# Second S buffer, spaced conversion steps and another conversion order in the first tile of an attention and feed-forward kernel

## The chip, the cores and the metric

The kernel runs on one core of one Trainium2 chip. The metric is device time in microseconds (us) of one execution; lower is better. An engine's instructions run in the order of its own queue, and an instruction waits at the head of that queue for what it needs, so that all behind it waits too. The engines are named as in the profile: PE (matmul), PEld (its weight loads), DVE (vector), ACT (scalar), POOL, and SP, which issues the DMAs.

## The reference, cut to what matters

```python
def _attn_ref(q, k, v, tau):                      # q, k, v: (4, 6080, 256)
    qn = q / (np.linalg.norm(q, axis=1, keepdims=True) + 1e-06)
    kn = k / (np.linalg.norm(k, axis=1, keepdims=True) + 1e-06)
    s = kn.transpose(0, 2, 1) @ qn / tau          # (4, 256, 256)
    a = softmax(s)                                # over the last axis
    return v @ a

def _moe_ref(x, w_in, w_out):                     # x: (24320, 256), d_ff 2048
    h = x @ w_in
    g = np.maximum(0.01 * h, h)
    return g @ w_out
```

`w_in` and `w_out` arrive as 64-bit floats; everything else is 32-bit.

## The kernel before, in words

For each of the 4 batches the kernel forms the 256x256 attention matrix, multiplies it into `w_in` (one 256x2048 weight per batch), and then runs `v` through this weight, the leaky step and `w_out`. Every operand of a matmul is split into a high and a low part, and a product is made of three passes (high-high, low-high, high-low), each a matmul of 128x128 by 128x512.

**Tiles and blocks.** The rows of a batch are cut into tiles of 1024. A tile passes through 8 blocks (the loop over `p`, 0 to 7). From tile 1 on a block is computed with seven weight combinations (A11, A12, A22 and the sums S1 to S4: a Strassen form, lines 978 to 1010). Tile 0, the first tile of the first batch, is computed directly (lines 963 to 975): a block has four products, C11 in bank x, C22 in bank y, C21 in bank z and C12 in bank x again. Each product has six matmuls (line 606). ACT then applies the leaky step out of the bank (`leaky`, line 617) and casts the high part (line 618), and DVE takes the low part (line 620). The products with `w_out` of a block (24 matmuls, line 653) are issued between the products of the next block in pieces of 5, 5, 8 and 6. Bank x is therefore wanted by C11 of the next block only 6 matmuls after C12 has filled it.

**Weights of the first batch.** The attention matrix times `w_in` is made in four pieces j = 0 to 3 of 512 columns, each of two halves h (`w_product`, line 421, six matmuls a half; here "W product"). Blocks 2j and 2j+1 of tile 0 use piece j: `direct_high` (ACT, line 433) and `direct_low` (DVE, line 437) copy it out of its bank into a buffer of the tag `w_split`. Pieces 2 and 3 also go to DRAM for later tiles, as all pieces do: `direct_store` stores the A parts, and `direct_sum` and `w_parts` (lines 443, 477) form S1 to S4 out of them, split them (ACT line 489, DVE line 490) into a tile `w_rest` with one buffer, and store that (line 502) once for each of the two blocks k = 0, 1 of the piece.

**Conversions.** The 64-bit weights are converted on the chip in pieces of 128x512 by seven steps (`f64_steps`): exponent (DVE, line 328), scaled (ACT, 333), tailed (ACT, 336), signed (DVE, 339 and 342), joined (DVE, 345 and 346), high part (ACT, 352) and low part (DVE, 355). A raw piece lies in one of four buffers (`raw`), which its low part frees. Four pieces of `w_in` are converted before tile 0; eight pieces `("wo", i)` of `w_out` and four `("win", j, h)` follow within it. Blocks 2j and 2j+1 need wo 2j+1, then wo 2j.

**The order.** Inside tile 0 the extra work stands in queues `todo` for "act", "dve", "pe" and "pe_late", as entries of a length, a function and a rank. `put` inserts by rank. After each product, `slot(queue, room)` issues entries from the front of a queue while the first one fits into the room. `steps_work` puts one step of a conversion and, once that is issued, the next one. `convert` and `direct_work` start conversions and S sums at given blocks. The recorded order is what each engine runs.

Of the kernel before, what the change touches and what calls it, by code (L numbers as in the profile page):

```python
# [10 lines left out]
F32R = mybir.dt.float32r  # L11
# [6 lines left out]
P = 128  # L18
# [13 lines left out]
def channel_attention_ffn(  # L32
# [36 lines left out]
    work = ctx.enter_context(tc.tile_pool(name="work", bufs=2))  # L69
# [4 lines left out]
    def bank(tag, bufs=1):  # L74
        return psum.tile([P, TW], F32, name="ps_" + tag, tag=tag, bufs=bufs)
# [15 lines left out]
    wo = [wo_hl[:, x:x + NF * C].rearrange("p (f d) -> p f d", d=C) for x in (0, NF * C + P)]  # L91
# [273 lines left out]
    win = {}  # L365
# [69 lines left out]
    def direct_low(j, h):  # L435
        hi, lo = w_direct[j, h]
        return nc.vector.tensor_tensor(out=lo, in0=a_sb[0, j, h], in1=f32(hi), op=ALU.subtract)
# [18 lines left out]
    def w_tmp(name):  # L456
        return work.tile([P, TW], F32, name=name, tag="w_tmp", bufs=4)
# [9 lines left out]
    def w_parts(b, j):  # L467

        HT = TW // 2
        a = [a_sb[b, j, h] for h in range(CH)]  # L470
        a21, a11, a22, a12 = a[0][:, 0:HT], a[0][:, HT:TW], a[1][:, 0:HT], a[1][:, HT:TW]
        s12, s34 = w_tmp("w_s"), w_tmp("w_s")
        s1, s2, s3, s4 = s12[:, 0:HT], s12[:, HT:TW], s34[:, 0:HT], s34[:, HT:TW]

        def sums(*of):
            for out, x, y, op in of:
                last = nc.vector.tensor_tensor(out=out, in0=x, in1=y, op=op)
            return last

        yield 0.8, lambda: sums((s1, a21, a22, ALU.add), (s3, a11, a21, ALU.subtract))  # L480
        yield 0.8, lambda: sums((s2, s1, a11, ALU.subtract), (s4, a12, s2, ALU.subtract))
        two = "p (s f) -> p s f"

        def split(k, to, at, *blocks):
            ks = slice(k * P, (k + 1) * P)
            for src, x0, n in blocks:
                src = src[:, ks] if n == 1 else src.rearrange(two, s=2)[:, :, ks]
                hi, lo = (x[:, x0 - at, :] if n == 1 else x[:, x0 - at:x0 - at + n, :] for x in to)
                (nc.vector.tensor_copy if b else nc.scalar.copy)(out=hi, in_=src)
                last = nc.vector.tensor_tensor(out=lo, in0=src, in1=f32(hi), op=ALU.subtract)  # L490
            return last

        for k in range(2):
            p, w = 2 * j + k, []

            def blocks(x0, n, name, w=w):

                w.append(work.tile([P, 2, n, P], F32R, name=name, bufs=1))
                return [w[-1][:, x] for x in range(2)]

            def store(x0, n, w=w, p=p):
                nc.sync.dma_start(
                    out=w_dram[b, p][:, :, x0 * P:(x0 + n) * P], in_=f32(w[-1].rearrange("p x s f -> p x (s f)"))
                )

            def begin(k=k, blocks=blocks, store=store):
                x0 = min(A11, A22)
                last = split(k, blocks(x0, 3, "w_first"), x0, (a11, A11, 1), (a[1], A22, 2))
                store(x0, 3)
                return last  # L510
# [160 lines left out]
    todo = {"act": deque(), "dve": deque(), "pe": deque(), "pe_late": deque(), "pe_next": deque()}  # L671
    steps = {}

    def at(w, fn, *args):
        steps.setdefault(w, []).append((fn, args))

    def slot(queue, room):
        engine = queue.split("_")[0]
        while todo[queue] and todo[queue][0][0] <= room:
            length, fn, _ = todo[queue].popleft()  # L680
            room -= length
            with in_order(engine):
                ins = fn()
            issued[engine] = ins

    def put(queue, length, fn, then=(), first=False):


        def run():
            ins = fn()  # L690
            for entry in then:
                if entry[0] == "call":
                    entry[1](*entry[2:])
                else:
                    put(*entry)
            return ins

        rank = 0 if first is True else first or 99
        at = 0 if first is True else sum(x[2] <= rank for x in todo[queue])
        todo[queue].insert(at, (length, run, rank))  # L700

    scores = [Scores(b, [G] * (NCHUNK // G)) for b in range(B)]

# [34 lines left out]
    def w_work(b, j, h=0):  # L738


        def taken():
            ins = w_taken(b, j, h)
            if h == 0:
                w_work(b, j, 1)
            else:
                for length, fn in w_parts(b, j):
                    put("dve", length, fn)
                if j + 1 < NWC:
                    length, fn, _ = todo["dve"].pop()
# [28 lines left out]
        put("dve", 0.7, lambda: direct_sum(j, 0), (), rank)  # L778
        put("dve", 0.7, lambda: direct_sum(j, 1), [("call", parts)], rank)

    def steps_work(rank, steps, then=()):
        (engine, length, fn), *rest = steps
        put(engine, length, fn, [("call", steps_work, rank, rest, then)] if rest else then, rank)

    def v_work(i, n0, n1, first=False):
        entries = v_entries[i][n0:n1]
        for length, fn in reversed(entries) if first else entries:
            put("dve", length, fn, (), first)

    v_entries, late = {}, {}  # L790

    def v_begin(i):
        v_entries[i] = list(v_parts(i))
# [2 lines left out]
    for i in range(NTILES):  # L796
        w = i * NPAIR
# [9 lines left out]
    conversions = deque([("wo", 1), ("wo", 0), ("win", 2, 0), ("win", 2, 1), ("wo", 2), ("wo", 3), ("win", 3, 0),  # L807
                         ("win", 3, 1), ("wo", 4), ("wo", 5), ("wo", 6), ("wo", 7)])
    loaded = deque()

    def convert_load(n=1):
# [5 lines left out]
    def convert(n):  # L817

        late["wanted"] = late.get("wanted", 0) + n
        while late["wanted"] and loaded:  # L820
            late["wanted"] -= 1
            of, steps = loaded.popleft()
            then = [("call", convert_load)]
            if len(of) == 2 and of[1] == CH - 1:
                then.append(("call", w_early, of[0], 0))
            late["rank"] = late.get("rank", 0) + 1
            steps_work(late["rank"], steps, then)

    for w, *calls in (
        (0, (convert, len(conversions) - 1), (direct_work, 0, 3, 3), (w_early, 1, 0)),  # L830
        (2, (direct_work, 1, 5, 9)),
        (6, (direct_work, 2, 50, 50)),
        (7, (direct_work, 3, 50, 50)),
    ):
        for fn, *args in calls:
            at(w, fn, *args)
# [83 lines left out]
    parts = [fn for _, fn in v_parts(0)]  # L920
    wo_first = [fn for engine, _, fn in loaded.popleft()[1]]
# [12 lines left out]
    ordered("dve", wo_first[0], parts[2], sc.turned_low)  # L934
    wo_first[1]()
    wo_first[2]()
    for h in range(CH):
        ordered("pe", lambda: w_product(0, 0, h, "yz"[h]))
        direct_high(0, h)
        ordered("dve", (parts[3], wo_first[4])[h], lambda: direct_low(0, h))  # L940
        if h == 0:
            ordered("dve", wo_first[3])
    fill(FILL * G)
    wo_first[5]()
    ordered("dve", wo_first[6])

    outs = []
# [9 lines left out]
    for i in range(NTILES):  # L957
        for p in range(NPAIR):
# [3 lines left out]
                fn(*args)  # L962
            if i == 0:
                for tag, (name, x, y), n in zip("xyzx", BLOCKS, (5, 5, 8, 24)):
                    ps = bank(tag)
                    direct_product(p, ps, x, y)
                    slot("act", 1.4)
                    out(n)
                    late["bank"] = "z" if tag == "x" else "y"
                    slot("pe_late", 0 if n == 5 else 1)  # L970
                    leaky(i, p, name, ps, temp(name="h"))
                    slot("act", 0.7)
                    slot("dve", 2.6)
# [68 lines left out]
```

## Time and profile before

| | |
|---|---|
| median of 3 runs | 2229.51 us (2229.44 to 2230.23) |
| the profiled execution, its own time | 2228.81 us |
| its span, first to last instruction | 2227.0 us |
| busy: PE, DVE, ACT | 98%, 66%, 66% |
| mean granted TensorE clock | 0.991 |
| tile 0 on PE, first product of block 0 to first product of tile 1 | 66.68 to 196.26 us |

The span is 1.81 us shorter than the execution's own time. Rows of the timeline give the start, the length, the engine, the line, the operation, what it writes and reads, the number of merged instructions, and in square brackets how long the engine had been idle and what released it. A row of the windows gives for a stretch its length and each engine's busy time (with the number of instructions), then the granted clock of PE, the DMA share and GB/s.

### The profile page before, as it was taken

The numbers are of one execution on the slowest core, as the hardware profiler recorded it, in microseconds if no ns is written. First come the engines' busy times: TensorE is split into PE (matmuls) and PEld (weight loads), VectorE is DVE, ScalarE is ACT, GpSimd is POOL, SyncE is SP. The second block draws the span as 40 slices with busy tenths as digits, with TensorE's granted clock in tenths as the row PEclk, the third lists the DMA queues.
The fourth block names the chain that finished last, engine by engine and source line by source line (L and its number), as shares of the span: only waits on it lengthen the run. The fifth ranks groups of instructions, "written<-read, shape, count | busy, mean of one in ns | idle before, by whom it ended". The sixth has DMA issues, their size and how long they took to land.

```text
span 2227.0 us, 27287 instructions
## 1 busy us (share of the span) xinstructions
PE 2177.6 (98%) x9960; PEld 1819.0 (82%) x9960; DVE 1464.8 (66%) x2572; ACT 1479.1 (66%) x2564; POOL 3.3 (0%) x11
## 2 busy tenths in 40 slices
PE   9787999999999999999999999999999999999999
PEld 7566888888888888888888888888888788888888
DVE  7666776766676766666767667667577555556554
ACT  6455777766667777776656777777666666666665
POOL 0000000000000000000000000000000000000000
PEclk9899999999999999999999999999999999999999
DMA  9535443442753434433465344343354432332331
GB/s 346 181 127 194 145 165 129 142 151 89 233 203 121 152 119 144 157 119 139 146 225 172 111 154 159 121 157 131 111 193 155 146 137 83 137 121 94 125 114 39
DMA packets 108533, 327.75 MB, mean 147 GB/s; under 512 B 10992, under 2 KB 29296, under 8 KB 108400
## 3 DMA queue, kind: packets, MB, share of 16 engines
q1 hardware_dynamic: 108400, 326.02, 42.7%
q8 instruction: 78, 1.28, 0.2%
q14 instruction: 55, 0.45, 0.1%
HBM read 267.52 MB, written 58.46 MB: 146 GB/s over the span
## 4 chain that ended last, share of the span: by engine, by line
PE 90%; DVE 4%; DMA 2%; ACT 2%; issue 1%; SPq 0%; ACTq 0%; DVEq 0%
PE ps_o L653 44%; PE ps_x L593 22%; PE ps_z L593 11%; PE ps_y L593 5%; PE ps_s L180 4%; PE ps_s L421 1%; DMA w_dram<-w_rest 1%; ACT h L617 1%; DVE g_split L620 1%; ACT g_split L618 1%; PE ps_x L606 1%; DVE h L627 1%; DMA qk_raw<-in_k_dram 1%; DVE sq_acc L140 0%; DVE w_rest L490 0%
## 5 line engine op out<-in xcount | busy, mean ns | idle before, releaser
L653 PE MATMUL ps_o<-g_split,w_out_split 128*128 128x512 f32 (+1 forms) x4608 | 1167.0, 389 | 0.7 <-DVE w_out_split L355 0.7
L653 PEld LDWEIGHTS ps_o<-g_split,w_out_split 128*128 128x128 f32 x4608 | 868.1, 188 | 177.0 <-DVE w_out_split L355 1.1
L620 DVE TENSOR_TENSOR g_split<-h,g_split 128x512 fp32r<-128x512 f32 (+1 forms) x768 | 525.2, 684 | 416.1 <-ACT g_split L618 413.2
L593 PE MATMUL ps_x<-v_split,w_split 128*128 128x512 f32 (+1 forms) x2208 | 621.3, 390 | 9.0 <-ACT h L633 9.0
L617 ACT ACTIVATE h<-h 128x512 f32<-128x512 f32 (+1 forms) x552 | 346.7, 628 | 273.8 <-DVE h L627 273.8
L633 ACT COPY h<-ps_x 128x512 f32<-128x512 f32 (+1 forms) x552 | 320.8, 581 | 280.3 <-PE ps_x L593 279.7
L618 ACT CAST g_split<-h 128x512 fp32r<-128x512 f32 (+1 forms) x768 | 473.5, 617 | 24.1
L593 PEld LDWEIGHTS ps_x<-v_split,w_split 128*128 128x128 f32 x2208 | 405.5, 189 | 83.1 <-ACT h L633 11.1
L627 DVE TENSOR_TENSOR h<-ps_z,h 128x512 f32<-128x512 f32 (+1 forms) x368 | 250.9, 682 | 262.4 <-ACT h L633 259.0
L593 PE MATMUL ps_z<-v_split,w_split 128*128 128x512 f32 (+1 forms) x1104 | 309.4, 388 | 5.7 <-DVE h L627 5.7
L593 PEld LDWEIGHTS ps_z<-v_split,w_split 128*128 128x128 f32 x1104 | 206.7, 188 | 49.7 <-DVE h L627 7.6
L593 PE MATMUL ps_y<-v_split,w_split 128*128 128x512 f32 (+1 forms) x552 | 154.7, 388 | 0.0
L627 DVE TENSOR_TENSOR h<-ps_y,h 128x512 f32<-128x512 f32 (+1 forms) x184 | 125.8, 684 | 1.3 <-PE ps_y L593 0.7
L617 ACT ACTIVATE h<-ps_x 128x512 f32<-128x512 f32 (+1 forms) x200 | 117.8, 589 | 11.9 <-PE ps_x L606 8.2
L180 PEld LDWEIGHTS ps_s<-qk_split 128*128 128x128 f32 x792 | 112.4, 190 | 11.1 <-issue 1.0
L593 PEld LDWEIGHTS ps_y<-v_split,w_split 128*128 128x128 f32 x552 | 103.8, 188 | 21.1 <-issue 0.5
L180 PE MATMUL ps_s<-qk_split 128*128 128x256 f32 x792 | 116.4, 283 | 0.0
L158 ACT CAST qk_split<-qk_raw 128x512 fp32r<-128x512 f32 x132 | 81.7, 619 | 45.2 <-PE ps_s L180 41.4
L553 DVE TENSOR_TENSOR v_split<-v_raw,v_split 128x512 fp32r<-128x512 f32 (+1 forms) x142 | 97.2, 686 | 4.5
L153 DVE TENSOR_TENSOR sq_acc<-sq_acc,sq 128x512 f32<-128x512 f32 x141 | 96.3, 683 | 0.0
L162 DVE TENSOR_TENSOR qk_split<-qk_raw,qk_split 128x512 fp32r<-128x512 f32 x132 | 90.3, 684 | 4.7 <-ACT qk_split L158 4.7
L150 ACT ACTIVATE sq<-qk_raw 128x512 f32<-128x512 f32 x141 | 88.6, 632 | 0.0
(116 smaller groups left out, 834.7 us busy)
## 6 DMA issues: line engine op xcount, KB each, us to landing
w_split<-w_dram SPq DMA_DIRECT2D x184, 896.0 KB, 4.7
qk_raw<-in_q_dram SPq DMA_DIRECT2D x92, 256.0 KB, 3.1
qk_raw<-in_k_dram SPq DMA_DIRECT2D x92, 256.0 KB, 3.7
v_raw<-in_vT_dram SPq DMA_DIRECT2D x40, 512.0 KB, 4.8
out_dram<-o_sb SPq DMA_DIRECT2D x80, 256.0 KB, 3.8
w_dram<-w_rest SPq DMA_DIRECT2D x32, 512.0 KB, 3.1
win<-win_dram SPq DMA_DIRECT2D x24, 512.0 KB, 4.2
w_dram<-w_first SPq DMA_DIRECT2D x24, 384.0 KB, 3.5
```

The lines of the kernel that those rows point to most:

```text
L150: return nc.scalar.activation(out=out, in_=self.chunk(j), func=AF.Square)
L153: return nc.vector.tensor_tensor(out=self.acc[0], in0=self.acc[0], in1=sq, op=ALU.add)
L162: return nc.vector.tensor_tensor(out=sp[:, :, 1, :], in0=self.chunk(j), in1=f32(sp[:, :, 0, :]), op=ALU.subtract)
L180: mm = nc.tensor.matmul(out=s, lhsT=lhsT, rhs=rhs, start=False, stop=last and n == len(passes) - 1, skip_group_check=True,)
L553: last = nc.vector.tensor_tensor(out=sp[:, 1, 0:w], in0=src, in1=f32(sp[:, 0, 0:w]), op=ALU.subtract)
L593: mm = nc.tensor.matmul(out=ps[:, 0:n], lhsT=w[:, x, a, :], rhs=sp[:, y, 0:n], start=first and k == 0, stop=k == 2, skip_group_check=True,)
L617: nc.scalar.activation(out=out[:, 0:n], in_=h[:, 0:n], func=AF.Prelu, alpha=0.01)
L618: issued["act"] = nc.scalar.copy(out=sp[:, 0, 0:n], in_=out[:, 0:n])
L620: issued["dve"] = nc.vector.tensor_tensor(out=sp[:, 1, 0:n], in0=out[:, 0:n], in1=f32(sp[:, 0, 0:n]), op=ALU.subtract)
L627: issued["dve"] = nc.vector.tensor_tensor(out=h[:, 0:n], in0=ps[:, 0:n], in1=h[:, 0:n], op=ALU.add)
L633: issued["act"] = nc.scalar.copy(out=h[:, 0:n], in_=ps[:, 0:n])
L653: issued["pe"] = nc.tensor.matmul(out=o_ps[i][j][h][:, 0:n], lhsT=wo[x][:, f, h * P:(h + 1) * P], rhs=sp[:, y, 0:n], start=p == 0 and earl ...
```

## The change

Three things are edited.

1. In `w_parts`, for the first batch (b = 0), the tile of block k = 1 comes from the tag `qk_split` (three buffers, which also hold the early converted `w_in` pieces of j = 3 and, later, splits of q and k). Block k = 0 keeps `w_rest`.
2. `late["tick"]` counts two to a product. Each queue entry has a tick from which it may be issued, and `slot` takes the first entry that is ready, instead of the first. A step of a conversion that changes engine becomes ready two ticks after the step before it was issued; a conversion that starts later than the loop's beginning waits four ticks for its first step. For conversions that start before the loop's first tick, the first three steps are issued at once.
3. The order of the conversions is another (wo 3 and 2 ahead of the win pieces), S sums of pieces 0 and 1 start later or at another rank, the rooms of block 0 are smaller, and in the lead-in the second `direct_low` stands ahead of the four DVE steps of the first conversion.

```diff
+                if b or k == 0:
+                    w.append(work.tile([P, 2, n, P], F32R, name=name, bufs=1))
+                else:
+                    w.append(work.tile([P, 2, n, P], F32R, name=name, tag="qk_split", bufs=3))
...
     def slot(queue, room):
-        while todo[queue] and todo[queue][0][0] <= room:
-            length, fn, _ = todo[queue].popleft()
-            room -= length
+        while True:
+            entry = next((x for x in todo[queue] if x[3] <= late["tick"]), None)
+            if entry is None or entry[0] > room:
+                return
...
-    def steps_work(rank, steps, then=()):
+    def steps_work(rank, steps, then=(), wait=0):
         (engine, length, fn), *rest = steps
-        put(engine, length, fn, [("call", steps_work, rank, rest, then)] if rest else then, rank)
+        follow = [("call", steps_work, rank, rest, then, 2 * (engine != rest[0][0]))] if rest else then
+        put(engine, length, fn, follow, rank, late["tick"] + wait)
...
-    conversions = deque([("wo", 1), ("wo", 0), ("win", 2, 0), ("win", 2, 1), ("wo", 2), ("wo", 3), ("win", 3, 0),
+    conversions = deque([("wo", 1), ("wo", 0), ("wo", 3), ("wo", 2), ("win", 2, 0), ("win", 2, 1), ("wo", 5), ("win", 3, 0),
...
+            begun = [] if late["tick"] else steps[:3]
+            for engine, _, fn in begun:
+                with in_order(engine):
+                    issued[engine] = fn()
...
-        (0, (convert, len(conversions) - 1), (direct_work, 0, 3, 3), (w_early, 1, 0)),
-        (2, (direct_work, 1, 5, 9)),
+        (0, (convert, len(conversions) - 1), (direct_work, 0, 6, 7), (w_early, 1, 0)),
+        (4, (direct_work, 1, 7, 50)),
...
+    ordered("dve", parts[3])
     for h in range(CH):
         ordered("pe", lambda: w_product(0, 0, h, "yz"[h]))
         direct_high(0, h)
-        ordered("dve", (parts[3], wo_first[4])[h], lambda: direct_low(0, h))
-        if h == 0:
-            ordered("dve", wo_first[3])
+        ordered("dve", lambda: direct_low(0, h))
...
+                    late["tick"] += 1
                     ps = bank(tag)
                     direct_product(p, ps, x, y)
-                    slot("act", 1.4)
+                    slot("act", 1.4 if p else 0.7)
...
                     leaky(i, p, name, ps, temp(name="h"))
-                    slot("act", 0.7)
-                    slot("dve", 2.6)
+                    late["tick"] += 1
+                    slot("act", 1.4)
+                    slot("dve", 2.6 if p else 1.5)
```

Below, the same instruction has a line number larger by 3 after the change (L617 becomes L620, L620 becomes L623, L653 becomes L656), and the numbers behind names tell buffers of one tag apart.

First place: DVE at the beginning of block 0. The two `w_split` low parts are those of piece 0; `f64_raw_442` is wo 1, and 450, 452, 454 and 456 are the next four pieces. Before:

```order
L437 TENSOR_TENSOR w_split_562<-ps_y_555,w_split_562 128x512
L339 SCALAR_TENSOR_TENSOR f64_scale_547<-f64_raw_442,f64_scale_547 128x512
L342 TENSOR_SCALAR f64_raw_442<-f64_raw_442 128x512
L345 SCALAR_TENSOR_TENSOR f64_raw_442<-f64_raw_442 128x512
L346 SCALAR_TENSOR_TENSOR f64_raw_442<-f64_raw_442,f64_scale_547 128x512
L437 TENSOR_TENSOR w_split_577<-ps_z_570,w_split_577 128x512
L355 TENSOR_TENSOR w_out_split_83<-f64_raw_442,w_out_split_83 128x512
L620 TENSOR_TENSOR g_split_605<-h_604,g_split_605 128x512
L328 TENSOR_SCALAR f64_scale_609<-f64_raw_450 128x512
L328 TENSOR_SCALAR f64_scale_611<-f64_raw_452 128x512
L328 TENSOR_SCALAR f64_scale_613<-f64_raw_454 128x512
```

After, at the same place:

```order
L437 TENSOR_TENSOR w_split_565<-ps_y_558,w_split_565 128x512
L437 TENSOR_TENSOR w_split_575<-ps_z_568,w_split_575 128x512
L339 SCALAR_TENSOR_TENSOR f64_scale_547<-f64_raw_442,f64_scale_547 128x512
L342 TENSOR_SCALAR f64_raw_442<-f64_raw_442 128x512
L345 SCALAR_TENSOR_TENSOR f64_raw_442<-f64_raw_442 128x512
L346 SCALAR_TENSOR_TENSOR f64_raw_442<-f64_raw_442,f64_scale_547 128x512
L355 TENSOR_TENSOR w_out_split_83<-f64_raw_442,w_out_split_83 128x512
L328 TENSOR_SCALAR f64_scale_589<-f64_raw_450 128x512
L328 TENSOR_SCALAR f64_scale_593<-f64_raw_452 128x512
L328 TENSOR_SCALAR f64_scale_597<-f64_raw_454 128x512
L328 TENSOR_SCALAR f64_scale_601<-f64_raw_456 128x512
L623 TENSOR_TENSOR g_split_621<-h_620,g_split_621 128x512
```

The second `direct_low` moved ahead of four conversion steps, and four exponent steps, the last of them on the fifth raw piece, now stand ahead of the low part of C11's leaky step. On ACT the eight steps scaled and tailed of these four pieces stand ahead of that leaky step likewise.

Second place: ACT where tile 0 ends and tile 1 begins (`w_s` holds two of S1 to S4 for piece 3; `h_1497` is C12 of block 7, `h_1528` the first product of tile 1). Before:

```order
L617 ACTIVATE h_1497<-ps_x_1484 128x512
L618 CAST g_split_1498<-h_1497 128x512
L633 COPY h_1528<-ps_x_1522 128x512
L150 ACTIVATE sq_acc_1518<-qk_raw_1271 128x512
L489 CAST w_rest_1478<-w_s_1452 128x256
L489 CAST w_rest_1478<-w_s_1453 128x256
L489 CAST w_rest_1502<-w_s_1452 128x256
L489 CAST w_rest_1502<-w_s_1453 128x256
L617 ACTIVATE h_1528<-h_1528 128x512
```

After, at the same place:

```order
L620 ACTIVATE h_1497<-ps_x_1484 128x512
L621 CAST g_split_1498<-h_1497 128x512
L489 CAST w_rest_1478<-w_s_1452 128x256
L489 CAST w_rest_1502<-w_s_1452 128x256
L489 CAST w_rest_1478<-w_s_1453 128x256
L489 CAST w_rest_1502<-w_s_1453 128x256
L636 COPY h_1528<-ps_x_1522 128x512
L150 ACTIVATE sq_acc_1518<-qk_raw_1266 128x512
L620 ACTIVATE h_1528<-h_1528 128x512
```

The four casts moved ahead of tile 1's first copy, and the two tiles they write are now in different buffers; before, `w_rest_1502` took the buffer that `w_rest_1478` had to leave first.

Third place: PE behind the second W product of piece 2 (`win_early` is the converted `w_in`, `aT` the attention matrix, and the number of `w_split` tells which half of which piece a product uses). Before, the product behind it is C11 of block 3:

```order
L421 MATMUL ps_z_920<-win_early_702,aT_545 128x512
L421 MATMUL ps_z_920<-win_early_790,aT_545 128x512
L606 MATMUL ps_x_942<-v_split_510,w_split_657 128x512 x3
L606 MATMUL ps_x_942<-v_split_531,w_split_686 128x512 x3
L653 MATMUL ps_o_704<-g_split_834,w_out_split_83 128x512 x3
```

After, it is C11 of block 4:

```order
L421 MATMUL ps_z_1004<-win_early_784,aT_545 128x512
L421 MATMUL ps_z_1004<-win_early_865,aT_545 128x512
L609 MATMUL ps_x_1033<-v_split_510,w_split_980 128x512 x3
L609 MATMUL ps_x_1033<-v_split_531,w_split_1016 128x512 x3
L656 MATMUL ps_o_698<-g_split_911,w_out_split_83 128x512 x3
```

Before, 657 and 686 are the two halves of piece 1, made long ago; after, 980 and 1016 are those of piece 2, and 1016 is copied out of the very bank z that the rows above fill. The W products of piece 3 moved from block 4 to block 5 in the same way.

More of the change, by code (lines that the diff above doesn't have):

```diff
@@ L494, in w_parts, with blocks @@
             p, w = 2 * j + k, []
-            def blocks(x0, n, name, w=w):
-                w.append(work.tile([P, 2, n, P], F32R, name=name, bufs=1))
+            def blocks(x0, n, name, k=k, w=w):
+                if b or k == 0:
+                    w.append(work.tile([P, 2, n, P], F32R, name=name, bufs=1))
+                else:
+                    w.append(work.tile([P, 2, n, P], F32R, name=name, tag="qk_split", bufs=3))
                 return [w[-1][:, x] for x in range(2)]
@@ L678, in slot, with put @@
         engine = queue.split("_")[0]
-        while todo[queue] and todo[queue][0][0] <= room:
-            length, fn, _ = todo[queue].popleft()
-            room -= length
+        while True:
+            entry = next((x for x in todo[queue] if x[3] <= late["tick"]), None)
+            if entry is None or entry[0] > room:
+                return
+            todo[queue].remove(entry)
+            room -= entry[0]
             with in_order(engine):
-                ins = fn()
+                ins = entry[1]()
             issued[engine] = ins
-    def put(queue, length, fn, then=(), first=False):
+    def put(queue, length, fn, then=(), first=False, ready=0):
         def run():
@@ L699, in put @@
         at = 0 if first is True else sum(x[2] <= rank for x in todo[queue])
-        todo[queue].insert(at, (length, run, rank))
+        todo[queue].insert(at, (length, run, rank, ready))
     scores = [Scores(b, [G] * (NCHUNK // G)) for b in range(B)]
@@ L748, in taken @@
                 if j + 1 < NWC:
-                    length, fn, _ = todo["dve"].pop()
+                    length, fn, *_ = todo["dve"].pop()
                     put("dve", length, fn, [("call", w_work, b, j + 1)])
@@ L788, in v_work @@
             put("dve", length, fn, (), first)
-    v_entries, late = {}, {}
+    v_entries, late = {}, {"tick": 0}
     def v_begin(i):
@@ L805, in channel_attention_ffn @@
                 at(max(NPAIR - 1 if p < 2 else NPAIR, w + p - 3), w_load, i, p)
-    conversions = deque([("wo", 1), ("wo", 0), ("win", 2, 0), ("win", 2, 1), ("wo", 2), ("wo", 3), ("win", 3, 0),
-                         ("win", 3, 1), ("wo", 4), ("wo", 5), ("wo", 6), ("wo", 7)])
+    conversions = deque([("wo", 1), ("wo", 0), ("wo", 3), ("wo", 2), ("win", 2, 0), ("win", 2, 1), ("wo", 5), ("win", 3, 0),
+                         ("wo", 4), ("win", 3, 1), ("wo", 7), ("wo", 6)])
     loaded = deque()
@@ L823, in convert @@
             then = [("call", convert_load)]
+            begun = [] if late["tick"] else steps[:3]
+            for engine, _, fn in begun:
+                with in_order(engine):
+                    issued[engine] = fn()
+            steps = steps[len(begun):]
             if len(of) == 2 and of[1] == CH - 1:
@@ L826, in convert @@
             late["rank"] = late.get("rank", 0) + 1
-            steps_work(late["rank"], steps, then)
+            steps_work(late["rank"], steps, then, 0 if begun else 4)
     for w, *calls in (
-        (0, (convert, len(conversions) - 1), (direct_work, 0, 3, 3), (w_early, 1, 0)),
-        (2, (direct_work, 1, 5, 9)),
+        (0, (convert, len(conversions) - 1), (direct_work, 0, 6, 7), (w_early, 1, 0)),
+        (4, (direct_work, 1, 7, 50)),
         (6, (direct_work, 2, 50, 50)),
@@ L939, in channel_attention_ffn @@
         direct_high(0, h)
-        ordered("dve", (parts[3], wo_first[4])[h], lambda: direct_low(0, h))
-        if h == 0:
-            ordered("dve", wo_first[3])
+        ordered("dve", lambda: direct_low(0, h))
     fill(FILL * G)
-    wo_first[5]()
+    ordered("dve", wo_first[3], wo_first[4])
+    issued["act"] = wo_first[5]()
     ordered("dve", wo_first[6])
```

## The prediction

> **What bounds the kernel now.** I read the page first, then the windows, one per block of tile 0, then PE's timeline and the list of waits.
>
> ```profile
> PE 2177.6 (98%) x9960; PEld 1819.0 (82%) x9960; DVE 1464.8 (66%) x2572; ACT 1479.1 (66%) x2564; POOL 3.3 (0%) x11
> PE   9787999999999999999999999999999999999999
> PEclk9899999999999999999999999999999999999999
> ```
>
> The kernel is bound by PE, which is idle for 2227.0 - 2177.6 = 49.4 us. Only the second to fourth slices (56 to 223 us) are below 9, and that is tile 0. The windows cut it at the first product of each block; the ninth row is tile 1's first block, the tenth its second, an undisturbed one.
>
> ```profile
> core 0: us, PE busy (x) PEld busy (x) DVE busy (x) ACT busy (x) POOL busy (x), PEclk, DMA share, GB/s
> 66.68:86.27 19.59, 12.59 (x39) 8.33 (x37) 12.14 (x21) 9.86 (x18) 0.00 (x0) 0.83 0.36 116
> 86.27:106.18 19.91, 12.82 (x48) 10.06 (x48) 12.23 (x25) 9.46 (x19) 0.00 (x0) 0.79 0.50 165
> 106.18:123.08 16.90, 16.43 (x61) 12.99 (x61) 11.11 (x19) 8.98 (x16) 0.00 (x0) 0.84 0.35 109
> 123.08:137.74 14.66, 11.48 (x49) 8.85 (x49) 11.17 (x20) 9.20 (x17) 0.00 (x0) 1.00 0.45 144
> 137.74:159.51 21.77, 15.85 (x60) 12.25 (x60) 11.49 (x22) 9.54 (x19) 0.52 (x1) 0.92 0.37 127
> 159.51:174.36 14.85, 12.71 (x49) 10.07 (x49) 11.02 (x18) 8.14 (x15) 0.00 (x0) 0.89 0.36 107
> 174.36:185.38 11.02, 11.02 (x48) 9.11 (x49) 7.28 (x14) 7.56 (x14) 0.00 (x0) 1.00 0.65 237
> 185.38:196.26 10.88, 10.88 (x49) 9.01 (x48) 8.39 (x15) 6.41 (x13) 0.00 (x0) 1.00 0.26 82
> 196.26:217.42 21.16, 12.12 (x47) 9.57 (x45) 8.79 (x18) 9.85 (x20) 0.00 (x0) 0.76 0.71 247
> 217.42:227.62 10.20, 10.20 (x47) 8.45 (x45) 7.46 (x13) 8.76 (x17) 0.00 (x0) 1.00 0.89 269
> ```
>
> Block 7 (10.88 us) runs without a gap: 48 matmuls at 0.227 us. Two W products add 12 x 0.227 = 2.7 us; block 0 has no `w_out` part, so 36 x 0.227 = 8.2 us. Without waits tile 0 would take 8.2 + 7 x 10.9 + 2 x 2.7 = 89.9 + 5.4, about 95 us. It takes 129.6, and tile 1's first block 11.0 more than its second. So about 34 + 11 = 45 us are lost, and no form of this change can gain more. PE's timeline shows where, the list of waits why:
>
> ```profile
> 70.46 1.12 PE L606 MATMUL ps_x<-v_split,w_split 128*128 128x512 f32 x2 [2.15 <-DVE w_split L437]
> 81.39 2.93 PE L421 MATMUL ps_z<-w_split,aT 128*128 128x512 f32 x6 [2.58 <-ACT h L617]
> 86.27 1.77 PE L606 MATMUL ps_x<-v_split,w_split 128*128 128x512 f32 x6 [1.94 <-ACT h L617]
> 106.18 2.93 PE L606 MATMUL ps_x<-v_split,w_split 128*128 128x512 f32 x6 [7.10 <-ACT h L617]
> 108.91 2.33 PE L653 MATMUL ps_o<-g_split,w_out_split 128*128 128x512 f32 x5
> 210.46 1.65 PE L593 MATMUL ps_x<-v_split,w_split 128*128 128x512 f32 x3 [9.04 <-ACT h L633]
> ```
>
> ```profile
> PE ps_x L606 <- ACT h L617: 16.8, 5, 7.1
> ACT w_out_split L352 <- DVE f_raw L346: 16.1, 6, 3.4
> ACT w_rest L489 <- DMA w_dram<-w_rest: 16.1, 3, 7.9
> ```
>
> PE waits for ACT to empty a bank. ACT is not busy: it stands at a high part (line 352) whose joined step DVE has not reached, 2.7 us a time, or at a cast into `w_rest` until the store of the tile before has landed, three times. After a long wait PE also runs at half clock: behind the one of 7.10 us six matmuls take 2.93 us.
>
> **The change part by part.** *The second S buffer.* Each of the three waits at line 489 lies between blocks k = 0 and 1 of a piece. With two tiles, k = 1 waits for nothing recent and k = 0 only for the store of the piece before, a block earlier; these stores landed in 3.0 to 7.4 us:
>
> ```profile
> DMA to landing us min/median/max: 3.0/5.2/7.4
> 206.81 0.71 ACT L489 CAST w_rest<-w_s 128x256 fp32r<-128x256 f32 x2 [7.95 <-DMA w_dram<-w_rest]
> ```
>
> The row at 206.81 is behind PE's 9.04 us at 210.46. Once gone, the four casts (two take 0.71, so 1.4 us) stand between C12's leaky step and tile 1's first copy. That copy then ends about 3.2 us after C12 on PE (leaky 1.2, casts 1.4, copy 0.6); the third product wants the bank 6 + 3 + 3 + 5 = 17 matmuls, 3.9 us, after C12. So nothing replaces the wait, and tile 1's first block falls to 10.2: **-11.0 us**. What the other two waits cost is within tile 0.
>
> *Block 0.* Its rows of DVE, ACT and SP, and the landing of a `w_in` piece:
>
> ```profile
> 67.20 0.68 DVE L339 SCALAR_TENSOR_TENSOR f_scale<-f_raw,f_scale 128x512 int32<-128x512 int32 x1
> 69.11 0.69 DVE L346 SCALAR_TENSOR_TENSOR f_raw<-f_raw,f_scale 128x512 f32<-128x512 f32 x1
> 69.72 0.68 DVE L437 TENSOR_TENSOR w_split<-ps_z,w_split 128x512 fp32r<-128x512 f32 x1
> 70.52 0.69 DVE L355 TENSOR_TENSOR w_out_split<-f_raw,w_out_split 128x512 fp32r<-128x512 f32 x1
> 71.41 0.43 SPq L317 DMA_DIRECT2D f_raw<-in_w_out_dram  x1
> 71.61 0.60 ACT L617 ACTIVATE h<-ps_x 128x512 f32<-128x512 f32 x1 [1.12 <-PE ps_x L606]
> 73.96 0.72 ACT L333 ACTIVATE f_scale<-f_scale,exp_bias 128x512 int32<-128x512 int32 x1 [1.10 <-DVE f_scale L328]
> 74.59 0.66 ACT L336 ACTIVATE f_raw<-f_raw 128x512 f32<-128x512 uint32 x1
> 83.93 0.59 ACT L433 CAST w_split<-ps_y 128x512 fp32r<-128x512 f32 x1 [1.94 <-PE ps_z L421]
> DMA to landing us min/median/max: 4.6/4.6/4.6
> ```
>
> The second low part moves from 69.72 to 67.2, so the 2.15 us wait goes and three products end at about 71.3. But the fifth piece's load is issued only when wo 1's low part has freed its buffer: that ends at 71.2 now and, 0.6 later behind the moved row, at 71.8. A load of `w_in` (now the fifth piece) lands 4.6 us after issue, at 76.5. Its exponent step stands at DVE's head, its two ACT steps ahead of all of block 0's leaky steps. So 76.5 + 0.42 + 0.7 + 0.6 = 78.2: C11's leaky step starts there, not at 71.61. Bank y is free 1.7 later, at 79.9; PE has then waited 8.6 us. Behind the 7.10 us wait six matmuls went from 106.18 to 108.91, 0.455 each, and the five behind them were as slow; for 11 such, W product, C12 and W product take 2.7 + 2.5 + 1.4 = 6.6, to 86.5. The cast at 83.93 shows that line 433 waits for the second W product, whose weights share the buffer; with the high part behind it and C12's leaky step that is 1.8 more. Block 1 starts at 88.3 instead of 86.27: block 0 takes **21.6** (now 19.59). Were the load to land at once, it would take 3.6 less; at 4.8, the slowest of the others, 0.2 more.
>
> *Blocks 1 to 7.* I followed DVE's and ACT's new rows with the durations of before. In block 1 the 7.1 us wait (store of `w_rest`, then the held high part) goes, since its casts now stand in block 3; the row at 86.27 shows that behind such a wait of 1.9 us the clock stays low, so 10.9 + 1.8 = **12.7**. A conversion now leaves a product between steps: take block 4. From the end of product y, PE has 5 + 6 + 8 + 6 + 6 = 31 matmuls, 7.0 us, until it wants bank x; on the other side stand one ACT step (1.0), y's leaky step (1.2), its low part (0.7), the four DVE steps (67.20 to 69.80: 2.6), the high part (0.65) and C12's leaky step (0.6): 6.75. It fits by 0.25, and by 0.25 to 0.8 at the other boundaries. So blocks 2 to 7 are at PE's pace, save where weights are now made just in time (third place of the order): behind the second W product PE has three matmuls (0.7) of the first half; ACT's cast 0.6 and DVE's low part 0.7 (as in the rows at 83.93 and 69.72) come later by 0.5 in block 4, and by 1.0 in block 6, where three other DVE rows stand ahead. Blocks 2 to 7: 10.9, 13.6, 11.4, 13.6, 11.9, 10.9.
>
> *Sum.* Tile 0: 21.6 + 12.7 + 10.9 + 13.6 + 11.4 + 13.6 + 11.9 + 10.9 = 106.6, against 129.6: -23.0. With -11.0 that is -34.0. For the boundaries that fit by 0.25 I allow 1.0 us (four misses of a quarter), so -33.0, and the profiled execution's 2228.81 becomes 2195.8; the median of the runs shown lies 0.7 above that execution, so **2196.5 us**. Later tiles run the same rows; the work is the same in number.
>
> [...] In the windows row below, 1.5 to 3.5 us behind the wait of only 2.15 us, the granted clock is 0.50.
>
> ```profile
> 72.00:74.00 2.00, 2.00 (x7) 1.51 (x6) 1.11 (x3) 0.87 (x3) 0.00 (x0) 0.50 0.79 219
> ```
>
> [...]
>
> **The rivals.** (a) *DVE and ACT set the pace, not PE.* For it: DVE's work in the first six blocks is 12.14 + 12.23 + 11.11 + 11.17 + 11.49 + 11.02 = 69.2 us, PE's 8.2 + 5 x 10.9 + 5.4 = 68.1, so margins are thin and half-clock stretches may follow each miss. Against: the conversions now spread over seven blocks. If half of tile 0's gain is lost, 2208; if all, 2228.81 - 11.0 + 0.7 = 2218.5. (b) *The second buffer does not do what it says*, because `qk_split` still holds a `w_in` piece of j = 3 or its store where k = 1 wants it: the 11 us at tile 1 stay, 2207.5. Against: those pieces are last read by the W products of block 5. (c) *Block 0's load lands early and nothing slips*: tile 0 near 97 us, 2185 to 2189. (d) *Slower.* In the new order a high part stands ahead of C12's leaky step in blocks 0 to 5. If DVE reaches each joined step late, PE waits at six boundaries. The change loses once a wait with its half clock costs over 45 / 6 = 7.6 us on average; at the worst of before (7.1, and 5.1 - 2.5 = 2.6 for the eleven matmuls behind it, so 9.7) it is 6 x 9.7 = 58 lost, not 45: 2242.5. Against it: five such waits took only 16.8 us together.
>
> **How the numbers follow.** My forecast (2189 to 2203) has 0.63, (a) 0.20, (b) 0.05, (c) 0.05, (d) 0.05, and 0.02 for a wash. The range takes the forecast, (b), half of (a) and part of (c): 2187 to 2211. No change means within 0.2%, 4.5 us, about what runs of this kernel can tell. Faster by more: forecast, (a), (b), (c), 0.93; same 0.02; slower 0.05.
>
> **What would show it.** In the profile after: no wait of ACT line 489 for a store near tile 1, its first block at about 10.2 us; in block 0 a PE wait of 8 to 9 us ahead of the first W product, with DVE idle until the fifth load lands; blocks 2 to 7 within a microsecond of the list. I am wrong if PE still waits over 2 us at any boundary from block 2 on, or if block 0 is shorter than 19 us.

## The result, and the profile after

The changed kernel takes 2192.18 us (median of 4 runs, 2190.28 to 2193.86), the kernel before beside it 2229.48 (4 runs, 2226.14 to 2230.23): a ratio of 0.9835, 95% interval 0.9818 to 0.9852. It is faster by 37.3 us or 1.7%; 2196.5 was predicted, with 2187 to 2211 as the range. The profiled execution took 2191.7 us. From its page, the span, the busy times, and PE and its clock in 40 slices:

```profile
span 2189.9 us, 27280 instructions
PE 2165.3 (99%) x9960; PEld 1811.4 (83%) x9960; DVE 1464.5 (67%) x2572; ACT 1477.5 (67%) x2564; POOL 3.3 (0%) x11
PE   9899999999999999999999999999999999999999
PEclk9999999999999999999999999999999999999999
```

Of the three slices below 9 one is left. The windows, cut as before at the first product of each block of tile 0 (eight rows), and then tile 1's first and second block:

```profile
core 0: us, PE busy (x) PEld busy (x) DVE busy (x) ACT busy (x) POOL busy (x), PEclk, DMA share, GB/s
66.25:86.85 20.60, 11.41 (x38) 8.26 (x37) 11.03 (x20) 10.83 (x20) 0.00 (x0) 0.75 0.33 107
86.85:97.86 11.01, 11.01 (x48) 9.12 (x49) 10.35 (x19) 7.11 (x12) 0.00 (x0) 1.00 0.41 115
97.86:109.26 11.40, 11.04 (x49) 8.82 (x47) 10.86 (x20) 8.92 (x17) 0.00 (x0) 1.00 0.56 184
109.26:123.04 13.78, 13.78 (x61) 11.37 (x61) 11.93 (x24) 9.61 (x18) 0.00 (x0) 1.00 0.66 208
123.04:134.71 11.67, 11.45 (x49) 8.93 (x48) 8.80 (x16) 9.32 (x16) 0.00 (x0) 1.00 0.45 138
134.71:148.31 13.60, 13.60 (x61) 11.27 (x60) 12.31 (x24) 8.88 (x18) 0.52 (x1) 1.00 0.52 176
148.31:159.98 11.67, 11.45 (x49) 8.93 (x48) 10.70 (x21) 7.26 (x14) 0.00 (x0) 1.00 0.86 286
159.98:170.86 10.88, 10.88 (x49) 9.01 (x48) 10.24 (x19) 7.36 (x14) 0.00 (x0) 1.00 0.56 193
170.86:181.41 10.55, 10.50 (x46) 8.37 (x45) 6.66 (x13) 8.94 (x19) 0.00 (x0) 1.00 1.01 375
181.41:191.91 10.50, 10.50 (x46) 8.34 (x45) 7.57 (x14) 8.95 (x17) 0.00 (x0) 1.00 0.93 331
```

Nearly all of the time still lost in tile 0 is in block 0: 20.60 us, in which PE is busy for 11.41, at a clock of 0.75. Tile 0 takes 170.86 - 66.25 = 104.61 us instead of 129.58, and tile 1's first block 10.55 instead of 21.16. The difference of the spans, 37.1 us, is 25.0 from tile 0, 10.6 from that block, 0.4 from a lead-in that ended earlier, less 0.3 in tile 1's second block; 1.4 are left for all the rest. Of the rows of PE's timeline in which it waited in tile 0, the three longest waits, with the row behind the first of them, and a wait at a later batch boundary:

```profile
78.67 2.93 PE L421 MATMUL ps_y<-w_split,aT 128*128 128x512 f32 x6 [7.62 <-ACT h L620]
81.40 2.59 PE L609 MATMUL ps_x<-v_split,w_split 128*128 128x512 f32 x6
86.85 1.66 PE L609 MATMUL ps_x<-v_split,w_split 128*128 128x512 f32 x6 [1.50 <-ACT h L620]
109.26 1.67 PE L609 MATMUL ps_x<-v_split,w_split 128*128 128x512 f32 x6 [0.36 <-ACT h L620]
1164.08 0.96 PE L596 MATMUL ps_z<-v_split,w_split 128*128 128x512 f32 x3 [2.00 <-DVE h L630]
1164.88 1.46 PE L656 MATMUL ps_o<-g_split,w_out_split 128*128 128x480 f32 x6
```

What stands behind the 7.62 us is in the timelines of SP, DVE and ACT: the fifth piece's load is issued at 71.40, its exponent step waits for it at DVE's head, two ACT steps follow, and only then C11's leaky step. But ACT is idle for only 0.41 us ahead of those two: from 71.75 to 75.32 it runs the six steps of the other begun pieces, the last of them at 74.68.

```profile
71.40 0.35 SPq L317 DMA_DIRECT2D f_raw<-in_w_in_dram  x1
75.27 0.43 DVE L328 TENSOR_SCALAR f_scale<-f_raw 128x512 int32<-128x512 int32 x1 [2.88 <-DMA f_raw<-in_w_in_dram]
74.68 0.64 ACT L336 ACTIVATE f_raw<-f_raw 128x512 f32<-128x512 uint32 x1
75.73 0.72 ACT L333 ACTIVATE f_scale<-f_scale,exp_bias 128x512 int32<-128x512 int32 x1 [0.41 <-DVE f_scale L328]
76.89 0.57 ACT L620 ACTIVATE h<-ps_x 128x512 f32<-128x512 f32 x1
```

The list of waits from 60 to 215 us no longer has ACT at the casts into `w_rest` for a store (16.1 us before), and ACT's waits for a joined step are fewer and shorter. Two rows of the list of before over the same stretch (total, times, longest), 29.4 us together:

```profile
ACT w_out_split L352 <- DVE f_raw L346: 21.6, 8, 3.4
ACT win_early L352 <- DVE f_raw L346: 7.8, 3, 2.7
```

The prediction's 16.1 us of waits for joined steps were the first of these two rows, counted from block 1 on. After the change the two are 9.5 us together:

```profile
ACT w_out_split L352 <- DVE f_raw L346: 6.3, 5, 3.4
ACT win_early L352 <- DVE f_raw L346: 3.2, 3, 1.3
```

### The profile page after: what moved, and what is told of

It is laid out like the page before. It is cut to its first block, busy times and chain, and to the rows that moved or that the text cites. A ratio compares the mean times of both kernels' runs of the same rounds, so it can differ in the third digit from the quotient of the medians.

```text
span 2189.9 us, 27280 instructions
## 1 busy us (share of the span) xinstructions
PE 2165.3 (99%) x9960; PEld 1811.4 (83%) x9960; DVE 1464.5 (67%) x2572; ACT 1477.5 (67%) x2564; POOL 3.3 (0%) x11
## 4 chain that ended last, share of the span: by engine, by line
PE 92%; DVE 4%; ACT 2%; DMA 1%; issue 1%; SPq 0%; ACTq 0%; DVEq 0%
PE ps_o L656 45%; PE ps_x L596 22%; PE ps_z L596 11%; PE ps_y L596 5%; PE ps_s L180 5%; PE ps_s L421 2%; DVE sq_acc L140 1%; PE ps_x L609 1%; DMA w_dram<-w_rest 1%; DVE h L630 1%; ACT h L620 1%; DVE g_split L623 1%; ACT g_split L621 0%; PE ps_y L421 0%; PE ps_y L609 0%
## 5 line engine op out<-in xcount | busy, mean ns | idle before, releaser
L656 PE MATMUL ps_o<-g_split,w_out_split 128*128 128x512 f32 (+1 forms) x4608 | 1161.8, 387 | 0.0
L656 PEld LDWEIGHTS ps_o<-g_split,w_out_split 128*128 128x128 f32 x4608 | 864.8, 188 | 174.3
L623 DVE TENSOR_TENSOR g_split<-h,g_split 128x512 fp32r<-128x512 f32 (+1 forms) x768 | 525.1, 684 | 394.2 <-ACT g_split L621 393.3
L620 ACT ACTIVATE h<-h 128x512 f32<-128x512 f32 (+1 forms) x552 | 346.6, 628 | 273.9 <-DVE h L630 273.9
L620 ACT ACTIVATE h<-ps_x 128x512 f32<-128x512 f32 (+1 forms) x200 | 117.6, 588 | 11.5 <-PE ps_x L609 8.1
```

The source lines that it names most:

```text
L620: nc.scalar.activation(out=out[:, 0:n], in_=h[:, 0:n], func=AF.Prelu, alpha=0.01)
L623: issued["dve"] = nc.vector.tensor_tensor(out=sp[:, 1, 0:n], in0=out[:, 0:n], in1=f32(sp[:, 0, 0:n]), op=ALU.subtract)
L656: issued["pe"] = nc.tensor.matmul(out=o_ps[i][j][h][:, 0:n], lhsT=wo[x][:, f, h * P:(h + 1) * P], rhs=sp[:, y, 0:n], start=p == 0 and earl ...
```

## The experiments

My theory: the second buffer takes away the waits for a store, the distances together with the order take away ACT's waits for joined steps, and the early beginnings put one new wait into block 0. The rivals: one of these parts does it all, or the new wait costs nothing because something else ends as late. Runs of one chip compare best by **the length of tile 0** (first product of block 0 to first product of tile 1 in PE's timeline), since it leaves out the lead-in and the later tiles: 129.58 us before, 104.61 after.

**The second buffer alone**, in the kernel before.

```diff
+                if b or k == 0:
                     w.append(work.tile([P, 2, n, P], F32R, name=name, bufs=1))
+                else:
+                    w.append(work.tile([P, 2, n, P], F32R, name=name, tag="qk_split", bufs=3))
```

> The kernel before with the second S buffer alone (nothing of the order moves but the casts of one piece). Theory (each of the three waits of ACT for a store of the first S tile goes, and PE's wait behind it with it): tile 1's first block falls from 21.2 to about 10.5, and in tile 0 the 7.1 us wait and the two waits of 1.3 and 4.6 us lose what the store cost ACT (3.7 and 4.4 us), so 2210 to 2214. Rival 1 (the held high parts are what binds tile 0, ACT then stands there instead): only tile 1's 11 us, 2218 to 2219. Rival 2 (the gain of the change is spacing, not the buffer): 2224 or more.

Measured: 2209.49 us (2208.16 to 2211.57), the kernel before on that chip 2226.3; ratio 0.9921 [0.9906, 0.9936]. Tile 0 takes 188.93 - 68.43 = 120.50. From the list of waits:

```profile
ACT w_out_split L352 <- DVE f_raw L346: 21.6, 8, 3.4
PE ps_x L609 <- ACT h L620: 13.5, 6, 3.6
```

No cast waits for a store any more. Tile 1's first block takes 199.34 - 188.93 = 10.41 us, and in tile 0 the buffer alone is worth 9.1. ACT's waits for joined steps are all still there: the first row is that of before. So the buffer does what it says, and about 17 us of the 37 need nothing else; the theory had 2210 to 2214.

**The change without the second buffer** (the four lines above taken back).

> The changed kernel with the S tile of block k = 1 back in the one buffer of k = 0. Theory (the buffer is worth as much within the new order as alone): tile 1's first block about 20 us again, and a wait of 3 to 5 us for a store on ACT in each of pieces 0 to 2, part of it reaching PE: 2205 to 2215. Rival (the spacing leaves ACT enough room that only tile 1's wait returns): 2201 to 2204.

Measured: 2217.33 us (2215.66 to 2221.3), ratio 0.9953 [0.9936, 0.997]. Tile 0 takes 116.57. The list of waits and PE's timeline:

```profile
ACT w_rest L489 <- DMA w_dram<-w_rest: 14.9, 3, 9.6
```

```profile
200.09 1.65 PE L593 MATMUL ps_x<-v_split,w_split 128*128 128x512 f32 x3 [11.63 <-ACT h L633]
```

Slower than either theory said. In the new order one buffer costs 25 us, not 11 to 17: the casts wait up to 9.6 us for the store, tile 0 loses 12.0, and tile 1's first block waits 11.63. The likely reason is that S sums start later in the new order, so that more of them fall together; that was not tried by itself.

**No distance** (every step is ready at once; order, rooms and buffer of the change stay).

```diff
-        todo[queue].insert(at, (length, run, rank, ready))
+        todo[queue].insert(at, (length, run, rank, 0))
```

> The changed kernel with every entry ready at once: order of the conversions, second buffer and the early first steps stay, the distance of a product between steps goes. Theory (the distance is what frees ACT from standing at high parts): waits of 2 to 4 us return at four or more block boundaries, 2203 to 2213. Rival (the other order of the conversions and the buffer do it all): 2190 to 2195.

Measured: 2212.44 us (2209.38 to 2213.79), ratio 0.9932 [0.9917, 0.9946]; tile 0 takes 121.62. The time is in the theory's range. ACT's waits for joined steps are back, 31.9 us, and PE waits over 2 us at three places from block 2 on (2.33, 2.37 and 4.71 us), where the theory had four or more:

```profile
ACT w_out_split L352 <- DVE f_raw L346: 20.0, 8, 3.4
ACT win_early L352 <- DVE f_raw L346: 11.9, 4, 3.3
```

**Half the distance** (one tick instead of two).

```diff
-... rest, then, 2 * (engine != rest[0][0]))] if rest else then
+... rest, then, 1 * (engine != rest[0][0]))] if rest else then
```

> A step that changes engine becomes ready one tick, half a product, after the step before it, instead of two. My theory (the distance keeps ACT from standing at a high part whose joining step is not done): half the distance covers less than a joined pair that stands behind other work of DVE, so the waits of ACT for the joining step rise from 9.5 us to 12 to 20, PE waits 2 us or more at one to three boundaries of blocks 1 to 7, and the time is 2194 to 2203. Rival (the order alone does it, and any distance over none is as good): the waits stay at 9 to 11 us, 2190 to 2194.

Measured: 2213.51 us (2211.54 to 2214.13), the kernel before on that chip 2227.16; ratio 0.9939 [0.9926, 0.9951]; tile 0 takes 122.36. Slower than my theory's range, with 29.2 us of such waits where it had 12 to 20, and no better than no distance. The waits of ACT in the run with one tick, and one of them in the timelines of DVE, ACT and PE:

```profile
ACT w_out_split L352 <- DVE f_raw L346: 19.1, 8, 3.4
ACT win_early L352 <- DVE f_raw L346: 10.1, 4, 3.3
```

```profile
110.77 0.69 DVE L339 SCALAR_TENSOR_TENSOR f_scale<-f_raw,f_scale 128x512 int32<-128x512 int32 x1
112.68 0.69 DVE L346 SCALAR_TENSOR_TENSOR f_raw<-f_raw,f_scale 128x512 f32<-128x512 f32 x1
113.41 0.65 ACT L352 CAST win_early<-f_raw 128x512 fp32r<-128x512 f32 x1 [2.10 <-DVE f_raw L346]
113.97 0.59 ACT L620 ACTIVATE h<-ps_z 128x512 f32<-128x512 f32 x1
114.61 0.96 PE L421 MATMUL ps_z<-win_early,aT 128*128 128x512 f32 x3 [4.30 <-ACT h L620]
```

The chain reads from the bottom up: PE wants bank z, its leaky step stands behind a high part, and that waits for a joined step recorded only half a product before it. DVE's four steps of a piece take 2.6 us (110.77 to 113.37), about what a product with its `w_out` matmuls takes (11 to 14 matmuls at 0.227 us, 2.5 to 3.2). In this run all twelve high parts waited, 2.4 us each on average; with the distance of the change eight did, 1.2 us each. The order, the rooms and the buffer without the distances give 14 us, no more than the buffer alone. No run has the distances in the old order, nor the new order, the later S sums or the rooms by themselves (the room of ACT behind a leaky step went from 0.7 to 1.4 in every block), so how much of the gain needs the new order as well stays open.

**The lead-in of before** (second low part of piece 0 again behind the four DVE steps of the first conversion).

```diff
         ordered("dve", lambda: direct_low(0, h))
+        if h == 0:
+            ordered("dve", wo_first[3], wo_first[4])
     fill(FILL * G)
-    ordered("dve", wo_first[3], wo_first[4])
```

> The changed kernel with the second low part of piece 0 back behind the four DVE steps of the first conversion: on all engines only these five rows of DVE change places. Theory (in block 0 the end of the fifth load sets when ACT gets to C11, and that hangs on the conversion, not on C11's product): PE waits 2.2 us in C11 again, but its wait ahead of the first W product is shorter by as much, and block 0 is 0 to 0.7 us shorter: 2191 to 2192.5. Rival (my step that the 2.15 us wait goes is a gain of its own): block 0 is 2 to 3 us longer, 2194 to 2196.

Measured: 2191.89 us (2191.59 to 2192.67), ratio 0.9842 [0.9827, 0.9856]: no difference in time, as the theory said. But the parts of the span moved. PE's timeline of this run:

```profile
70.73 1.12 PE L609 MATMUL ps_x<-v_split,w_split 128*128 128x512 f32 x2 [2.15 <-DVE w_split L437]
79.42 1.65 PE L421 MATMUL ps_y<-w_split,aT 128*128 128x512 f32 x6 [3.64 <-ACT h L620]
85.29 1.65 PE L609 MATMUL ps_x<-v_split,w_split 128*128 128x512 f32 x6 [1.49 <-ACT h L620]
1162.95 1.51 PE L596 MATMUL ps_z<-v_split,w_split 128*128 128x512 f32 x3 [2.45 <-DVE h L630]
1164.25 2.52 PE L656 MATMUL ps_o<-g_split,w_out_split 128*128 128x480 f32 x6
```

The old wait of 2.15 us is back, and the wait ahead of the W product is 3.64 instead of 7.62. The W product starts 79.42 - 66.95 = 12.47 us after block 0 in this run and 78.67 - 66.25 = 12.42 after the change: taking the 2.15 us away is worth nothing, since ACT's steps of the begun pieces, the fifth piece's last of all, set that moment either way (C11's leaky step starts 10.70 us after block 0 here and 10.64 after the change). What differs is the clock. Here it was 0.50 for 3.4 us behind the first wait, where PE would have waited anyway, and 1.00 behind the second (1.65 us for six matmuls, where 2.93 were taken after), so block 0 and tile 0 (102.30) are 2.3 us shorter than after, where the theory had at most 0.7. Most of that is given back far from the edit: at the second batch boundary PE waited 2.45 us here and 2.00 after, and the nine matmuls of the two rows there took 4.03 instead of 2.42.

**The changed kernel again**, as a base for the three kernels beside it.

> The changed kernel, word for word, once more, as the base for the three kernels beside it. 2190 to 2194 us; tile 1 starts within 0.3 us of 170.86 and the waits of PE in tile 0 are the same. What differs from run to run should come from the batch boundaries, where PE waits 1.5 to 2.5 us in every kernel and the clock was halved behind such a wait in some profiles (a row of 0.50 for about 3 us, some 1.6 us more) and not in others.

Measured: 2193.73 us (2190.0 to 2195.83), ratio 0.985 [0.9836, 0.9863]. Tile 0 takes 105.07, with the same waits. But tile 1 starts at 174.51, not at 170.86: block 0 starts at 69.44 instead of 66.25. Of these 3.2 us 1.7 are the clock in the lead-in, which from 50 to 60 us was 0.83 on average, against 1.00 in the first profile: the same twenty matmuls took 4.56 us in the first profile of the changed kernel and 6.25 in this one. The other 1.5 had been lost before that.

```profile
51.80 4.56 PE L180 MATMUL ps_s<-qk_fill 128*128 128x256 f32 x20
53.32 6.25 PE L180 MATMUL ps_s<-qk_fill 128*128 128x256 f32 x20
```

I had put all of the spread on the batch boundaries, and the clock was 1.00 behind all three of them in both profiles; the lead-in makes up to 3 us of it.

**The fifth piece not begun early** (three begun conversions instead of four).

```diff
-            begun = [] if late["tick"] else steps[:3]
+            begun = [] if late["tick"] or late.get("rank", 0) >= 3 else steps[:3]
```

> Only the first three of the four conversions begin with three steps at once, so the exponent of the fifth piece and its two steps on ACT no longer stand ahead of the leaky steps of block 0. My theory (the fifth load at the head of DVE and ACT sets block 0): C11's leaky step starts behind the third pair of ACT steps, at 75.3 instead of 76.9, the first W product at 77.1 instead of 78.7, block 0 takes 19.0 instead of 20.6, tile 1 starts 1.6 earlier, and the time is 2190 to 2191.5. Rival (what is not begun early is late afterwards): ACT's high part of that piece waits for its joining step, PE waits 2 us or more at a boundary of blocks 1 to 5, tile 1 starts no earlier, 2192 to 2196.

Measured: 2192.37 us (2191.63 to 2195.46), ratio 0.9847 [0.9834, 0.9861]. By its time it can't be told from the changed kernel; it lies above the theory's 2190 to 2191.5, where the rival had put it. In PE's timeline the wait is 1.69 us shorter than the 7.62, which is the 1.6 of the theory. What goes is ACT's 0.41 us of waiting for the load and its two steps of that piece, 1.16, so the run doesn't show the load alone:

```profile
79.56 2.93 PE L421 MATMUL ps_y<-w_split,aT 128*128 128x512 f32 x6 [5.93 <-ACT h L620]
87.31 1.65 PE L609 MATMUL ps_x<-v_split,w_split 128*128 128x512 f32 x6 [1.50 <-ACT h L620]
```

Block 0 takes 87.31 - 68.82 = 18.49, tile 0 102.06, and the late wait that the rival needs is not there. The profiled execution hides the gain: its lead-in is 2.6 us longer than the first profile's, and the clock fell to 0.50 for 3.4 us at each of two batch boundaries.

**One begun conversion, and the lead-in of before.**

```diff
-            begun = [] if late["tick"] else steps[:3]
+            begun = [] if late["tick"] or late.get("rank", 0) >= 1 else steps[:3]
...
         ordered("dve", lambda: direct_low(0, h))
+        if h == 0:
+            ordered("dve", wo_first[3], wo_first[4])
```

> Only one conversion begins with three steps at once, and the second low part of piece 0 stands behind the four DVE steps, as before the change. My theory: PE reaches the W product at 75.8, as in the run with the lead-in of before, and the leaky steps of C11 and C22, behind one pair of ACT steps instead of four, are done by 74.9, so the wait of 3.64 goes and block 0 takes 14.7 instead of 18.3; with nothing late afterwards tile 1 starts at about 165.6 and the time is 2186 to 2189. Rival: three conversions begin a block later, so their joining steps come late, ACT waits 2 to 3.4 us for one of them at two or more boundaries of blocks 1 to 4, tile 1 starts at 168 to 174, 2189 to 2196.

Measured: 2185.37 us (2185.05 to 2189.75), ratio 0.9819 [0.9805, 0.9832], the fastest of all, 8.4 us below the changed kernel beside it; their intervals do not overlap. Between the two profiled executions tile 0 makes 6.7 us and the lead-in another 2.9. Against the run with the lead-in of before only the begun conversions differ, so the gain is theirs: 2191.89 to 2185.37 us, and tile 0 from 102.30 to 98.39. The windows of blocks 0 and 1 and of the rest of tile 0, and the rows of PE's waits in block 0:

```profile
66.52:80.26 13.74, 9.40 (x38) 6.50 (x36) 9.93 (x18) 7.29 (x14) 0.00 (x0) 1.00 0.51 161
80.26:91.65 11.39, 11.18 (x48) 8.93 (x49) 10.27 (x20) 10.25 (x21) 0.00 (x0) 1.00 0.40 112
91.65:164.91 73.26, 72.28 (x313) 58.43 (x313) 65.06 (x120) 51.38 (x92) 0.52 (x1) 1.00 0.59 197
```

```profile
70.30 0.73 PE L609 MATMUL ps_x<-v_split,w_split 128*128 128x512 f32 x2 [2.15 <-DVE w_split L437]
74.39 1.66 PE L421 MATMUL ps_y<-w_split,aT 128*128 128x512 f32 x6 [0.62 <-ACT h L620]
```

Block 0 is 13.74 instead of 20.60, the wait ahead of the W product 0.62. The rival's late joined steps did not show: blocks 2 to 7 take 73.26, against 73.00 after. Tile 0 is 98.39 us, and for 92.86 of them PE is busy.

## Why the prediction was right, and where it was off

**What bounds it.** Right: PE. But the sum for a tile 0 without waits counted W products twice: 8.2 + 7 x 10.9 + 2 x 2.7 is 89.9 by itself, since block 0's 8.2 holds its own two. So about 51 us were to be had, not 45, and rival (d) needed waits of 51 / 6 = 8.5 us, not 7.6; the forecast itself does not use these figures. The run with one begun conversion recovers 31.2 us in tile 0 and 10.0 in tile 1's first block (11.15 us), 41.2 in all.

**The second buffer.** Right: -11.0 was said, -10.6 measured, and nothing took the wait's place. That it is also worth 9.1 us in tile 0 by itself the prediction did not separate.

**Block 0.** Right within a microsecond, 21.6 said and 20.60 measured. The load landed in 3.8 us, not 4.6 (my term was the first of the two `w_in` loads in tile 0 of before, issued at 93.2 and 108.5 us, which landed in 4.6 and 4.8), and was issued 0.4 earlier; so C11's leaky step stands at 76.89, not 78.2, and PE waited 7.62, not 8.6. From the first W product to block 1 the sum had 8.4 us, the trace 8.18. But the load is not what holds this block up. ACT was idle for only 0.41 us ahead of the fifth piece's steps, since the six steps of the three other begun pieces, which the prediction put at nothing, kept it busy to 75.32; so "were the load to land at once, it would take 3.6 less" comes to 0.4 in this trace. With one begun piece the W product starts 7.87 us after block 0, with three 10.74, with four 12.42. That the block came out so near is in part luck: the load and those steps ended within half a microsecond of each other.

**Block 1.** The step that failed: "the row at 86.27 shows that behind such a wait of 1.9 us the clock stays low", hence 12.7. Measured 11.01: the wait was 1.50 us and the clock 1.00. In the kernel before the clock was 1.00 in the 1.94 us of the wait ahead of that row, fell to 0.50 some 1.4 us behind its start and stayed there for 3.41 us. So 1.8 us was the right price of that wait, but one such row does not make a rule for the next wait: of the waits up to 1.79 us in the table below only one stood with a half clock behind it, and of those of 1.82 to 2.37 us 16 of 26.

**Blocks 2 to 7.** 72.3 said, 73.0 measured, no single one off by over 0.5. The waits for low parts in blocks 4 and 6 are 0.22 each instead of 0.5 and 1.0, and one of 0.36 stands at the end of block 2.

**The sum.** Against the 2195.8 of the profiled execution the measured 2191.7 is: block 0 -1.0, block 1 -1.7, blocks 2 to 7 +0.7, the allowance not needed -1.0, tile 1's first two blocks +0.7, the lead-in -0.4, the rest -1.4: together -4.1. The last term fits the clock, not the change: in PE's timeline of the kernel before, the row behind a wait of 2.17 us at the third batch boundary took 1.97 us, where the same six matmuls after the change took 1.46 at the second one (the row at 1164.88) and no row at the others was slow.

```profile
1738.17 0.96 PE L593 MATMUL ps_z<-v_split,w_split 128*128 128x512 f32 x3 [2.17 <-DVE h L627]
1738.97 1.97 PE L653 MATMUL ps_o<-g_split,w_out_split 128*128 128x480 f32 x6
```

**The half clock.** Behind block 0's long wait the matmuls from 78.67 us on ran at a granted clock of 0.50 for 5.0 us, which costs 2.5, as in my sum. The prediction's row of 0.50 behind a wait of 2.15 us is one of the 16 in the second row of the table below; behind the wait of as much in the run with one begun conversion the clock was 1.00.

**The rivals.** (a) did not come: from block 2 on PE waits 0.36 + 0.22 + 0.22 = 0.8 us in all, at a clock of 1.00. The runs with no distance and with one tick, 2212 and 2213.5, lie in the times that it gave, through ACT's waits for joined steps; so it was the right thing to fear. (b) is excluded by the windows after: tile 1's first block takes 10.55 us, and no cast waits for a store. (c) did not come either: the load landed 0.8 us sooner than said, and block 0 still waited; the run with one begun conversion reaches its figures by another way (tile 0 near 97 and 2185 to 2189 were said, 98.39 and 2185.37 measured). (d) had no sign; without distances PE waited over 2 us at three places from block 2 on, 4.71 us at the longest, short of what it needed.

## What to carry to other kernels

A step that hands over to another engine needs a distance of what the first engine has queued for it (here 2.6 us, a product with its output matmuls); here half of it was worth no more than none. Whatever is begun early must not put an instruction that waits for a late load at the head of a queue that frees banks, nor a run of steps that keeps that queue busy when the bank is wanted: here four begun pieces instead of one held the W product of block 0 back by 4.5 us, of which ACT waited 0.41 for the load. Count the load's issue, not only its length (here it was issued 5.15 us into block 0 and landed 3.8 us later). Where gains are below 3 us, compare the stretch that was changed, since here lead-in and clock moved the whole time by as much (block 0 started 3.2 us apart in two profiles of the same kernel).

## What the runs showed of the hardware

The table takes every wait of PE of 1.3 us and more in tile 0, tile 1's first blocks and at the batch boundaries, in all ten profiles, and counts those with a granted clock of 0.50 behind them (read in steps of 0.5 us):

| PE idle for | waits | clock 0.50 behind |
|---|---|---|
| 1.31 to 1.79 us | 21 | 1 (in a chain of waits, clock already halved) |
| 1.82 to 2.37 us | 26 | 16 (in two the clock was already halved) |
| 2.45 to 4.71 us | 15 | 14 (not behind the 3.64 of the lead-in run) |
| 5.93 us and more | 9 | 9 |

In 19 of the 30 half clocks of the second and third rows the clock stayed at 0.50 for 3.41 or 3.42 us, so I put such a wait at 1.7 us more than itself (an estimate, half of 3.41); behind the long waits of block 0 (5.93 to 7.70 us) it lasted 3.1 to 6.1 us from PE's return. Behind the shorter waits it began up to about 1.5 us after PE had resumed. The lead-in, which the table leaves out, has a half clock behind a wait of only 1.31 us in the second profile of the changed kernel (the twenty matmuls of 6.25 us) and none behind the one of 0.50 us at the same place in the first; eight matmuls of a single column follow each of these waits, and what part they have in it no run here shows. The length of a wait alone does not tell whether the clock falls: behind 14 waits of 1.82 to 2.37 us it went from full to half, and behind ten others of that row it stayed at 1.00. Why the 3.64 us wait left the clock alone stays open.
